# A fused attention and SoLU kernel: the last mantissa bits of eight float64 weight pieces taken by ScalarE, and a new table of places

## The chip, the cores and the metric

One core of one Trainium2 chip runs the whole program. The metric is the device time of one execution in microseconds. TensorE is called PE here, its weight loads PEld, VectorE DVE, ScalarE ACT, GpSimd POOL, and SyncE, which issues every DMA of this kernel, SP.

## What is computed

The reference, cut to what matters (8 batches, 8 heads, 576 rows, head size 64, 32 packed rows; 4608 tokens, model size 512, inner size 1024):

```python
p_packed = sm_attn(p, k, v)              # softmax attention of 32 packed rows over 576
out = sm_attn(q, p_packed, p_packed)     # 576 rows over the 32 packed ones
x = out as 4608 x 512
h = x @ w_in                             # 512 -> 1024
e = exp(h - max(h)); sm = e / sum(e)
solu = h * sm
ln = (solu - mean) / sqrt(var + 1e-6) * g_ln
return ln @ w_out                        # 1024 -> 512
```

Both weight matrices arrive as float64. A float64 number is two 32-bit words: the upper one holds the sign, the exponent and 20 bits of the mantissa, the lower one the other 32, of which a float32 needs the first three.

## The kernel before

**Weights.** Each matrix is cut into four pieces of 128 partitions x 1024 numbers (1 MB of float64). Pieces 0 to 3 are `w_in` (loads `lw0` to `lw3`), 4 to 7 are `w_out` (loads `lW0` to `lW3`). A piece goes through five steps: `wa` (ACT, line 229) takes the exponent bits of the upper words, `wl` (`last_bits`, lines 231 to 237) takes the last three bits out of the lower words, `wm` (DVE, line 242) joins both into a magnitude, `wp` (PE, line 252) adds up columns of the magnitudes, and `ws` (DVE, line 259) puts the sign in and frees the piece's buffers. Two buffers `e` hold the results of `wa` and two buffers `u` those of `wl`, so `wa` of a piece waits until `ws` of the piece two before has let its buffer go. `WL_BY` says for each piece which engine does `wl`: POOL on line 235 or ACT on line 237.

When the four pieces of `w_out` are through, `pw` (lines 335 to 341, DVE) computes their scale `gs`; then eight chunks are split into two float16 parts each (`dg`, `ch`, `cl` on ACT, `cm` on PE, lines 355 to 372). When those of `w_in` are through, `wb` (line 263) computes their scale, and `zx`, `zw`, `zy` (lines 292, 295, 299 on POOL, ACT, POOL) split them.

**Attention.** For each block (batch) b: `kt`, `qt` transpose keys and queries on DVE (line 468; in block 0 PE does it, `ka`, `qa`, with copies `kc`, `qc` on ACT); `s1`, `mx`, `ex` are the first softmax; `tp`, `tc`, `av`, `pp` make the packed rows; `sx`, `sb`, `sm`, `su`, `se`, `ss`, `sn`, `at`, `ah`, `al` the second softmax in two float16 parts; `z`, `zh`, `zl` multiply the packed rows by `w_in` in place of the 576 rows, so that `h` is later a product with inner size 32 per head.

**Token tiles.** 36 tiles of 128 tokens: `m1` (PE, line 765, 12 products of 512 columns), `nm`, `bd`, `u`, `yl` on DVE (lines 771 to 803), `ex`, `yh`, `sq`, `ev` on ACT, `mu`, `ca`, `cr` on POOL, `tr` (SP, line 807), a DMA that transposes `y` for the second product, `m2a` and `m2b` (PE, line 829, 12 products each), `st` (SP, line 836), the store.

**What sets the order.** The string `ORDER` lists every step once, as name/block, name/w for weights, or name-tile. `perform` walks it: it issues the first step of the list whose predecessors are issued and whose buffers are free. Each engine and the queue of SP then run their instructions strictly in the order of issue, so a step that waits holds up all that stands behind it on its engine. `h` has two PSUM buffers, `pa` four, `raw` (keys, queries and two of the weight pieces) three, `yT` two.

```python
def last_bits(n):
    ...
    if WL_BY[n] == 'p':
        nc.gpsimd.tensor_scalar(out=last_of[n], in0=words, scalar1=LAST, ...)
    else:
        nc.scalar.activation(last_of[n], words, AF.Copy, scale=LAST)
```

Of the kernel before, what the change touches and what calls it, by code (L numbers as in the profile page):

```python
# [36 lines left out]
cl6/w cm0/w ko/w wl2/w dg4/w wa3/w wl3/w dg2/w lP/w lk0/1 lk1/1 lk2/1 lk3/1 lv0/1 lk0/2 wm2/w wp2/w ws2/w cm2/w sm0/0
su0/0 se0/0 sm1/0 su1/0 wm3/w wp3/w ws3/w z0/0 z1/0 ss0/0 sn0/0 cl0/w ch1/w cl7/w pa/w se1/0 dg3/w ch5/w cm4/w cm3/w
wb/w un/0 ss1/0 at0/0 zh1/0 zh0/0 dg5/w ah0/0 dg1/w pd/w zx1/w uq/0 sn1/0 at1/0 ah1/0 cm5/w cl5/w cl3/w cm1/w cl4/w
cl1/w cl2/w al0/0 al1/0 zx2/w zl0/0 zl1/0 m1-0 px/w kt0/1 kt1/1 kt2/1 kt3/1 lk1/2 lk2/2 lk3/2 s10/1 s11/1 m1-3 nm-0  # L40
mx0/1 bd-0 mx1/1 ex-0 u-0 nm-3 ex0/1 ex1/1 zw1/w kt0/2 es0/1 kt1/2 kt2/2 bd-3 kt3/2 mu-0 gd/w zx0/w zx3/w ca-0 tp0/1
tp1/1 tp2/1 m1-2 tc0/1 tc1/1 tc2/1 ex-3 zw2/w zw3/w u-3 zy1/w mu-3 yh-0 s10/2 s11/2 m1-1 lq0/1 lv1/1 lq1/1 lq2/1 lv2/1
lq3/1 mx0/2 es1/1 yl-0 ex0/2 mx1/2 rs/1 tr-0 yh-3 yl-3 sq-3 ex1/2 av/1 pp/1 pt/1 tp0/2 tp1/2 sq-0 tc0/2 zw0/w tc1/2
qt0/1 pc/1 qt1/1 pe/1 qt2/1 qt3/1 m2a-0 pk/1 sx0/1 to/1 nm-2 un/1 nm-1 sb0/1 sm0/1 ph/1 pl/1 bd-1 zy2/w cr-0 ca-3
zy3/w cr-3 zy0/w su0/1 m2b-0 tp2/2 sx1/1 sb1/1 sm1/1 es0/2 ex-1 su1/1 ca-1 ev-0 tc2/2 se0/1 ss0/1 sn0/1 uq/1 z0/1
zh0/1 zl0/1 se1/1 ss1/1 lk0/3 lk1/3 lv0/2 tr-3 lk2/3 lv1/2 lv2/2 st-0 lk3/3 lq0/2 lq1/2 m2a-3 z1/1 av/2 m2b-3 at0/1
u-1 ah0/1 zh1/1 sn1/1 at1/1 ah1/1 al0/1 mu-1 al1/1 yh-1 ex-2 bd-2 es1/2 zl1/1 yl-1 u-2 kt0/3 kt1/3 kt2/3 kt3/3 m1-7
m1-4 sq-1 mu-2 ca-2 nm-7 rs/2 s10/3 mx0/3 pp/2 yh-2 ev-3 yl-2 ex-7 ex0/3 lq2/2 tr-1 lq3/2 lk0/4 st-3 lk1/4 lk2/4 tr-2
lq0/3 lq1/3 lk3/4 m2a-1 qt0/2 s11/3 mx1/3 m2b-1 bd-7 pe/2 u-7 ca-7 uc-4 mu-7 ex1/3 sq-2 cr-2 pt/2 tp0/3 tp1/3 tc0/3
pc/2 nm-4 m1-5 qt1/2 qt2/2 qt3/2 nm-5 bd-4 tp2/3 tc1/3 yh-7 ex-4 yl-7 sq-7 ex-5 u-4 m2a-2 m2b-2 cr-1 mu-4 ev-1 bd-5  # L50
kt0/4 kt1/4 kt2/4 kt3/4 ev-2 u-5 m1-8 pk/2 yh-4 tc2/3 to/2 sx0/2 lv0/3 lv1/3 tr-7 lq2/3 lq3/3 st-1 s10/4 m1-6 es0/3
sb0/2 un/2 mx0/4 yl-4 sm0/2 ex0/4 ph/2 nm-6 ca-4 mu-5 su0/2 cr-7 m2a-7 s11/4 pl/2 bd-6 mx1/4 yh-5 se0/2 sq-4 m2b-7
ex1/4 ev-7 ex-6 sx1/2 yl-5 ss0/2 sb1/2 es0/4 sm1/2 st-2 lv2/3 av/3 tr-4 st-7 lv0/4 tr-5 zz/1 zz/0 z0/2 m2a-4 m2b-4
su1/2 cr-4 zh0/2 se1/2 sq-5 es1/3 rs/3 u-6 pp/3 mu-6 ev-4 zl0/2 ss1/2 qt0/3 qt1/3 pt/3 z1/2 ca-6 ca-5 cr-5 sn0/2 at0/2
pc/3 zh1/2 sn1/2 yh-6 ah0/2 m2a-5 nm-8 pe/3 bd-8 at1/2 ah1/2 ex-8 qt2/3 zl1/2 u-8 qt3/3 pk/3 m2b-5 tp0/4 es1/4 rs/4
yl-6 uq/2 al0/2 al1/2 m1-10 mu-8 sq-6 to/3 yh-8 tc0/4 ev-5 lk0/5 lv1/4 lk1/5 lq0/4 lq1/4 lk2/5 tr-6 st-5 lq2/4 lk3/5
sx0/3 sx1/3 m1-12 nm-10 yl-8 sb0/3 sb1/3 nm-12 un/3 bd-10 ex-10 u-10 bd-12 tp1/4 sq-8 ex-12 tp2/4 m2a-6 m2b-6 uq/3
cr-6 ca-8 tc1/4 tc2/4 ph/3 ca-12 mu-10 pl/3 kt0/5 kt1/5 cr-8 ev-6 yh-10 kt2/5 kt3/5 sm1/3 u-12 sm0/3 mu-12 su1/3 su0/3
m1-11 tr-8 lq3/4 st-4 lv2/4 z0/3 s10/5 zh0/3 mx0/5 ex0/5 zl0/3 yl-10 yh-12 m1-9 av/4 s11/5 nm-11 yl-12 sq-12 bd-11
mx1/5 nm-9 pp/4 es0/5 ex1/5 bd-9 es1/5 m2a-8 m2b-8 tp0/5 tp1/5 ex-11 se0/3 ss0/3 se1/3 tc0/5 pe/4 ss1/3 ev-8 sq-10  # L60
ca-10 sn0/3 u-11 at0/3 st-6 lk0/6 lq0/5 lk1/6 tr-10 lk2/6 lk3/6 kt0/6 uc-13 cr-10 sn1/3 mu-11 ex-9 tc1/5 cr-12 ca-11
lq1/5 tr-12 m2a-10 z1/3 m2b-10 lv0/5 lq2/5 lv1/5 lv2/5 st-8 ah0/3 zh1/3 ca-9 al0/3 qt0/4 qt1/4 zl1/3 at1/3 qt2/4 kt1/6
qt3/4 yh-11 yl-11 u-9 m2a-12 tp2/5 m2b-12 pt/4 ah1/3 ev-10 ev-12 al1/3 mu-9 tc2/5 sq-11 yh-9 m1-16 rs/5 kt2/6 pc/4
kt3/6 pk/4 yl-9 to/4 sq-9 sx0/4 s10/6 nm-16 sb0/4 mx0/6 ex-16 m1-14 nm-14 un/4 bd-16 bd-14 ex0/6 ex-14 lq3/5 lq0/6
st-12 tr-11 lq1/6 st-10 tr-9 m2a-11 m2b-11 u-14 cr-11 mu-14 m1-17 yh-14 u-16 sm0/4 yl-14 su0/4 ph/4 se0/4 ev-11 sq-14
nm-17 ss0/4 bd-17 m1-13 sx1/4 av/5 sb1/4 s11/6 mu-16 yh-16 yl-16 ex-17 ca-17 mx1/6 u-17 pp/5 pe/5 nm-13 es0/6 pl/4
bd-13 sm1/4 ex1/6 lk0/7 lq2/6 lq3/6 tr-14 m2a-14 m2b-14 zz/2 z0/4 pt/5 m1-15 zz/3 pc/5 mu-17 sn0/4 ca-16 at0/4 yh-17
sq-16 cr-16 ca-14 zh0/4 ex-13 zl0/4 su1/4 se1/4 ss1/4 sn1/4 cr-14 pk/5 to/5 nm-15 uq/4 yl-17 bd-15 sq-17 ah0/4 ev-14
al0/4 qt0/5 es1/6 un/5 tp0/6 m2a-9 m2b-9 tc0/6 z1/4 tr-16 lk1/7 lv0/6 st-11 lk2/7 lv1/6 lv2/6 st-14 tr-17 ex-15 zh1/4
qt1/5 at1/4 ah1/4 u-13 mu-13 ca-13 cr-9 ev-9 yh-13 rs/6 u-15 mu-15 al1/4 m2a-16 m2b-16 tp1/6 ev-16 tc1/6 ph/5 qt2/5  # L70
zl1/4 qt3/5 pl/5 yl-13 m1-19 z0/5 sx0/5 nm-19 zh0/5 zl0/5 sb0/5 m1-18 yh-15 nm-18 yl-15 sq-15 bd-18 m2a-17 tp2/6 sx1/5
tc2/6 sb1/5 av/6 sm0/5 sm1/5 pp/6 z1/5 zh1/5 ex-18 lk3/7 kt0/7 pe/6 u-18 kt1/7 m2b-17 st-9 tr-13 kt2/7 kt3/7 zl1/5
bd-19 st-16 m2a-13 m2b-13 cr-17 su0/5 ca-15 sq-13 cr-13 ev-17 ex-19 ca-18 mu-18 yh-18 su1/5 yl-18 se0/5 se1/5 ss1/5
u-19 uq/5 ev-13 m1-20 s10/7 s11/7 m1-21 mx0/7 ss0/5 sn0/5 sn1/5 mu-19 sq-18 ex0/7 es0/7 nm-20 mx1/7 ex1/7 ex-20 st-13
tr-15 tr-18 lq0/7 st-17 nm-21 at1/5 yh-19 ah1/5 cr-15 uc-22 m2a-15 m2b-15 tp0/7 pt/6 m2a-18 m2b-18 al1/5 bd-20 at0/5
ah0/5 al0/5 qt0/6 qt1/6 yl-19 es1/7 qt2/6 pc/6 u-20 cr-18 mu-20 ca-19 bd-21 sq-19 yh-20 yl-20 m1-25 pk/6 ev-18 ex-21
tc0/7 ev-15 qt3/6 u-21 to/6 sq-20 sx0/6 sx1/6 un/6 sb0/6 sm0/6 m1-23 lv0/7 lq1/7 lv1/7 lq2/7 lq3/7 tr-20 tr-19 st-18
lv2/7 mu-21 nm-23 nm-25 bd-23 ph/6 ex-23 u-23 mu-23 cr-19 ca-20 m2a-20 m2b-20 tp1/7 yh-21 yh-23 yl-21 sb1/6 sm1/6
qt0/7 yl-23 bd-25 m1-24 sq-23 sq-21 ex-25 nm-24 bd-24 ex-24 tc1/7 u-25 tr-21 st-15 m2a-19 m2b-19 tp2/7 m1-22 m2a-21
m2b-21 mu-25 cr-20 yh-25 u-24 ca-25 su0/6 su1/6 ca-21 mu-24 uq/6 ev-19 tc2/7 ev-20 se0/6 yl-25 sq-25 cr-21 av/7 nm-22  # L80
pl/6 ss0/6 rs/7 sn0/6 ca-23 qt1/7 bd-22 st-19 tr-23 zz/4 z0/6 m1-26 ex-22 se1/6 ss1/6 sn1/6 u-22 at0/6 ah0/6 ev-21
zh0/6 pp/7 pe/7 al0/6 cr-25 pt/7 tr-25 st-21 st-20 zz/5 zl0/6 pc/7 at1/6 qt2/7 qt3/7 mu-22 cr-23 m2a-23 pk/7 z1/6
yh-22 to/7 zh1/6 un/7 nm-26 yl-22 ph/7 pl/7 zl1/6 ah1/6 yh-24 sq-22 ex-26 al1/6 bd-26 yl-24 u-26 m2a-25 m2b-25 m2b-23
ev-23 ev-25 tr-22 st-25 tr-24 m1-29 z0/7 sx0/7 m1-27 zh0/7 nm-29 sb0/7 sx1/7 bd-29 zl0/7 sb1/7 sm1/7 mu-26 ca-22 cr-22
uq/7 yh-26 yl-26 sq-26 sq-24 ex-29 sm0/7 su0/7 m2a-24 m2b-24 ca-24 nm-27 ex-27 bd-27 ca-27 cr-24 ev-24 se0/7 u-29
ss0/7 ca-29 mu-29 m2a-22 m2b-22 yh-29 su1/7 sn0/7 yl-29 at0/7 u-27 z1/7 zh1/7 m1-28 tr-26 nm-28 zl1/7 tr-29 se1/7
m1-30 m2a-29 m2a-26 m2b-26 m2b-29 ss1/7 mu-27 sq-29 cr-29 st-24 ex-28 yh-27 ah0/7 bd-28 nm-30 yl-27 sq-27 u-28 bd-30
sn1/7 at1/7 ex-30 ah1/7 mu-28 al0/7 al1/7 ca-28 uc-31 ev-29 u-30 mu-30 yh-30 m1-35 yl-30 nm-35 tr-27 st-23 yh-28 yl-28
sq-28 m1-34 sq-30 st-29 tr-30 m2a-27 m2b-27 m2a-30 nm-34 bd-35 ex-34 ex-35 bd-34 u-34 u-35 m1-32 cr-27 ev-22 mu-35
ca-35 ca-26 cr-26 ca-30 ev-26 yh-35 yl-35 sq-35 st-22 tr-35 m2b-30 m1-31 nm-32 ex-32 bd-32 u-32 mu-32 yh-32 yl-32  # L90
nm-31 sq-32 ex-31 ev-27 m2a-35 m1-33 m2b-35 zz/7 zz/6 tr-28 st-26 st-27 tr-32 m2a-28 m2b-28 m2a-32 m2b-32 ca-32 cr-35
bd-31 ca-31 cr-28 u-31 ev-35 mu-31 yh-31 yl-31 sq-31 st-35 mu-34 cr-30 ev-30 st-30 yh-34 nm-33 tr-31 m2a-31 m2b-31
ex-33 yl-34 bd-33 u-33 mu-33 cr-32 yh-33 yl-33 sq-33 ca-33 cr-33 tr-34 m2a-34 m2b-34 ev-32 ev-28 st-28 tr-33 ca-34
st-32 m2a-33 m2b-33 sq-34 cr-34 ev-34 st-34 cr-31 ev-31 st-31 ev-33 st-33
# [836 lines left out]
```

## Time and profile before

| | us |
|---|---|
| median of 3 runs | 423.75 |
| the 3 runs | 423.5, 423.75, 427.74 |
| the profiled execution, its own time | 421.8 |
| its span, first to last instruction | 420.0 |

The profile records one execution. Its span is 1.8 us shorter than the time of the same execution, and that execution is 1.95 us faster than the median. The page of the profile gives the busy time of each engine, a picture of the span in 40 slices, the chain of work that ended last, and groups of equal instructions with their mean duration and the idle time before them. The trace behind it can be asked for single instructions in order of time, for waits, and for the busy time of each engine in any stretch.

### The profile page before, as it was taken

To read this page: it belongs to the slowest core of one execution; us is meant where nothing else is said; L and a number is where in the kernel's file an instruction comes from. 1 tells how busy PE (TensorE), PEld (TensorE's weight loads), DVE (VectorE), ACT (ScalarE), POOL (GpSimd) and SP (SyncE) were. 2 spreads that over 40 slices of the span, in tenths; PEclk is the share of its full clock that TensorE was granted. 3 is DMA by queue.
4 is the path that set the end of the run, shared out by engine and by line. 5 is a ranking of instruction groups with operands and counts; after the bars stand their busy time and mean duration, and the time that the engine had idled before them with its cause. 6 is when DMAs were issued, how large, how long until landed. Compare 5 with 4: busy or idle time off the path is not lost.

```text
span 420.0 us, 8360 instructions
## 1 busy us (share of the span) xinstructions
PE 383.5 (91%) x3176; PEld 183.8 (44%) x3176; DVE 328.9 (78%) x661; ACT 246.6 (59%) x440; POOL 184.8 (44%) x293
## 2 busy tenths in 40 slices
...
GB/s 206 383 385 96 217 112 197 135 209 203 105 214 210 178 195 185 208 179 245 218 133 99 233 119 2 215 190 123 122 107 52 76 88 40 150 25 127 175 148 78
DMA packets 243384, 67.00 MB, mean 160 GB/s; under 512 B 216464, under 2 KB 236944, under 8 KB 242832
## 3 DMA queue, kind: packets, MB, share of 16 engines
...
## 4 chain that ended last, share of the span: by engine, by line
PE 49%; DVE 21%; DMA 9%; SPq 6%; POOL 6%; issue 5%; ACT 3%; DVEq 0%; ACTq 0%; POOLq 0%
PE pa L829 32%; PE h L765 11%; DMA yT<-yhl 5%; POOL u L235 3%; SPq L452 2%; DMA zh<-in_moe_w_in_dram 2%; DVE yhl L803 2%; DVE nm L771 2%; DVE u L792 2%; POOL w_in_sb L292 2%; DVE s L597 2%; DVE zl L654 1%; PE pa L634 1%; SPq L807 1%; DVE mx L601 1%
## 5 line engine op out<-in xcount | busy, mean ns | idle before, releaser
L829 PE MATMUL pa<-wch,yT 128*128 128x512 f16 x576 | 178.6, 382 | 4.0 <-DMA yT<-yhl 2.8
L829 PEld LDWEIGHTS <-yT 128*128 128x128 f16 x864 | 83.3, 98 | 109.4 <-issue 7.7
L829 PE MATMUL pa<-wcl,yT 128*128 128x512 f16 x288 | 109.7, 381 | 0.0
L803 DVE SCALAR_TENSOR_TENSOR yhl<-u,negmu,yhl 128x1024 f16<-128x1024 f32 x36 | 47.1, 1309 | 21.5 <-ACT yhl L800 15.2
L787 ACT ACTIVATE e<-h,bias,unit 128x1024 f32<-128x1024 f32 x36 | 43.3, 1203 | 27.4 <-DVE bias L773 13.0
L765 PE MATMUL h<-zh,a2h 128*128 128x512 f16 (+1 forms) x160 | 54.9, 381 | 2.1 <-DVE u L792 2.1
L765 PE MATMUL h<-zh,a2l 128*128 128x512 f16 (+1 forms) x160 | 54.7, 379 | 0.1
L765 PE MATMUL h<-zl,a2h 128*128 128x512 f16 (+1 forms) x160 | 54.7, 379 | 0.0
L800 ACT ACTIVATE yhl<-u,negmu 128x1024 f16<-128x1024 f32 x36 | 41.1, 1145 | 16.9 <-POOL negmu L796 11.3
L792 DVE SCALAR_TENSOR_TENSOR u<-e,s_row,h 128x1024 f32<-128x1024 f32 x36 | 45.1, 1259 | 3.5 <-ACT e L787 3.0
L771 DVE TENSOR_REDUCE nm<-h 128x1 f32<-128x1024 f32 x36 | 43.6, 1211 | 5.1 <-PE h L765 5.1
L796 POOL TENSOR_SCALAR negmu<-su 128x1 f32<-128x1 f32 x36 | 8.8, 244 | 88.0 <-DVE u L792 71.8
L833 ACT ACTIVATE o_sb<-pa,c_row 128x512 f32<-128x512 f32 x36 | 24.3, 683 | 39.0 <-PE pa L829 15.9
L765 PEld LDWEIGHTS <-a2h 128*128 128x128 f16 (+1 forms) x320 | 27.7, 100 | 37.5 <-issue 9.3
L811 ACT ACTIVATE e<-u,negmu 128x1024 f32<-128x1024 f32 x36 | 41.1, 1143 | 0.0
L604 POOL TENSOR_TENSOR s<-s,mx 128x576 f32<-128x576 f32 x16 | 20.5, 1289 | 35.4 <-DVE mx L601 29.5
L617 POOL TENSOR_TENSOR a<-a,sm 128x576 f32<-128x576 f32 x16 | 19.2, 1207 | 22.0 <-DVE sm L614 9.9
L673 POOL TENSOR_TENSOR a2l<-s,a2h 128x576 f16<-128x576 f32 x16 | 21.7, 1356 | 10.1 <-ACT a2h L669 7.4
L509 ACT ACTIVATE e<-pa,nmx 128x288 f32<-128x288 f32 x28 | 13.7, 494 | 16.6 <-DVE nmx L498 12.9
L649 ACT ACTIVATE zh<-pa 128x512 f16<-128x512 f32 x28 | 15.2, 594 | 12.2 <-PE pa L634 12.2
L765 PEld LDWEIGHTS <-a2l 128*128 128x128 f16 (+1 forms) x160 | 14.4, 100 | 17.1 <-POOL a2l L673 0.6
L822 POOL TENSOR_TENSOR c_row<-c_row,neg_half 128x1 f32<-128x1 f32 x36 | 20.0, 555 | 3.0
...
## 6 DMA issues: line engine op xcount, KB each, us to landing
...
```

Of the source, the lines that this page charges most:

```text
L604: by('su', r).tensor_tensor(out=st['w', r], in0=st['w', r], in1=st['mx', r].unsqueeze(2).broadcast_to([P, NB, J]), op=ALU.subtract)
L673: by('al', r).tensor_tensor(out=lo, in0=a2T, in1=hi, op=ALU.subtract)
L765: nc.tensor.matmul(h[rows, 512 * n:512 * n + 512], lhsT=lhsT, rhs=z[:, r, 512 * n:512 * n + 512], start=t == 0, stop=t == end)
L771: nc.vector.tensor_reduce(out=nm, in_=st['h'], axis=AX.X, op=ALU.max, negate=True)
L787: nc.scalar.activation(st['e'], st['h'], AF.Exp, bias=st['bias'], scale=st['unit'][:, 1:2], accum_out=st['se'])
L792: nc.vector.scalar_tensor_tensor(out=st['u'], in0=st['e'], scalar=st['s_row'], in1=st['h'], op0=ALU.mult, op1=ALU.mult, accum_out=st['su'])
L800: nc.scalar.activation(st['y'][:, 0], st['u'], AF.Identity, bias=st['negmu'])
L803: nc.vector.scalar_tensor_tensor(out=st['y'][:, 1], in0=st['u'], scalar=st['negmu'], in1=st['y'][:, 0], op0=ALU.add, op1=ALU.subtract)
L811: nc.scalar.activation(st['e'], st['u'], AF.Square, bias=st['negmu'], accum_out=st['sq'])
L822: nc.gpsimd.tensor_tensor(out=c_row, in0=c_row, in1=neg_half, op=ALU.pow)
L829: nc.tensor.matmul(st['po'], lhsT=st['yT'][:, a, c], rhs=w[:, c], start=c == 0 and t == 0, stop=c == NFC - 1 and t == 2)
L833: nc.scalar.activation(st['o'], st['po'], AF.Copy, scale=st['c'])
```

## The change

The table of who does `wl` changes from POOL to ACT for all eight pieces, and the string `ORDER` is replaced as a whole; the work itself is the same. In the head of the program the loads now begin with `lk/0 lg/w lW0/w lp/w lW1/w lW2/w lW3/w`, so the queries of block 0 (`lq/0`) come behind all four pieces of `w_out`, and the first piece to be worked on is 4. Of the 63 lines of the table two are shown.

```diff
-WL_BY = 'pppppppp'
+WL_BY = 'aaaaaaaa'
 ORDER = '''
-lk/0 lp/w lq/0 lW1/w lw0/w lg/w lW0/w lW3/w ka0/0 ka1/0 kc0/0 kc1/0 ka2/0 p0/w ka3/0 kc2/0 kc3/0 s10/0 mx0/0 s11/0
+lk/0 lg/w lW0/w lp/w lW1/w lW2/w lW3/w ka0/0 ka1/0 gm/w kc0/0 kc1/0 wa4/w ka2/0 ka3/0 kc2/0 wl4/w kc3/0 wa5/w wl5/w
...
```

In the three places below, `e` and `u` are the buffers of `wa` and `wl`, `zh`, `zl` and `raw` the buffers a weight piece is loaded into, `yT` and `yhl` what `ws` writes for `w_out`, `w_in_sb` what it writes for `w_in`.

ACT near the start of the program, before: the exponentials of block 0 (line 509) stand ahead of every weight step of this engine, and line 237 does not occur.

```order
L158 COPY kT<-h 128x2x2x128
L160 COPY kT<-h 128x64
L158 COPY kT<-h 128x2x2x128
L160 COPY kT<-h 128x64
L509 ACTIVATE e_229,es<-h,nmx 128x288 x4
L229 ACTIVATE e<-zh 128x1024
L158 COPY qT<-h 128x2x2x128
L160 COPY qT<-h 128x64
L229 ACTIVATE e<-zh 128x1024
L158 COPY qT<-h 128x2x2x128
L160 COPY qT<-h 128x64
L229 ACTIVATE e<-raw 128x1024
```

ACT at the same place, now:

```order
L229 ACTIVATE e<-raw 128x1024
L158 COPY kT<-h 128x2x2x128
L160 COPY kT<-h 128x64
L237 ACTIVATE u<-raw 128x1024
L158 COPY kT<-h 128x2x2x128
L160 COPY kT<-h 128x64
L229 ACTIVATE e<-zh 128x1024
L237 ACTIVATE u<-zh 128x1024
L229 ACTIVATE e<-raw 128x1024
L237 ACTIVATE u<-raw 128x1024
L509 ACTIVATE e_260,es<-h,nmx 128x288 x4
L535 COPY e1T<-pa 128x512 x2
```

Three pieces, each with its `wa` and `wl`, now stand ahead of the exponentials of block 0.

DVE from the scale `gs` on, before:

```order
L341 TENSOR_SCALAR gs<-g_sb,w_scale 128x8
L259 SCALAR_TENSOR_TENSOR yT<-raw,e 128x1024
L551 TENSOR_SCALAR pp<-pa,rs 128x128 x2
L556 TENSOR_REDUCE peak<-pp 128x1
L565 COPY ppT<-pa 128x256
L242 SCALAR_TENSOR_TENSOR e<-e,u 128x1024
L597 STREAM_TRANSPOSE s_464<-h 128x288 x2
L597 STREAM_TRANSPOSE s_467<-h 128x288 x2
L259 SCALAR_TENSOR_TENSOR w_in_sb<-zl,e 128x1024
L242 SCALAR_TENSOR_TENSOR e<-e,u 128x1024
L259 SCALAR_TENSOR_TENSOR w_in_sb<-zh,e 128x1024
```

DVE from the scale `gs` on, now:

```order
L341 TENSOR_SCALAR gs<-g_sb,w_scale 128x8
L242 SCALAR_TENSOR_TENSOR e<-e,u 128x1024
L514 TENSOR_REDUCE ssum<-es 128x1 x2
L259 SCALAR_TENSOR_TENSOR w_in_sb<-zh,e 128x1024
L518 TENSOR_SCALAR rs<-ssum 128x2
L519 RECIPROCAL rs<-rs 128x2
L551 TENSOR_SCALAR pp<-pa,rs 128x128 x2
L565 COPY ppT<-pa 128x256
L556 TENSOR_REDUCE peak<-pp 128x1
L597 STREAM_TRANSPOSE s_467<-h 128x288 x2
L601 TENSOR_REDUCE mx<-s_467 128x18
L242 SCALAR_TENSOR_TENSOR e<-e,u 128x1024
```

Before, piece 0 was through and the sums of the first softmax (lines 514 to 519) were done ahead of `gs`; now these come behind it, and the sign step of piece 6, which came behind it, is done.

SP between the transposes (`tr`) of tiles 5, 6 and 8, before (the first row is `tr-5`, the second transpose `tr-6`, the last row `tr-8`):

```order
L807 DMA_TRANSPOSE yT<-yhl 128x16x128
L452 DMA raw<-in_k_dram 32x72x32
L458 DMA v_sb<-in_v_dram 128x8x128
L452 DMA raw<-in_k_dram 32x72x32
L452 DMA raw<-in_q_dram 32x72x32 x2
L452 DMA raw<-in_k_dram 32x72x32
L807 DMA_TRANSPOSE yT<-yhl 128x16x128
L836 DMA out_dram<-o_sb 128x512
L452 DMA raw<-in_q_dram 32x72x32
L452 DMA raw<-in_k_dram 32x72x32
L807 DMA_TRANSPOSE yT<-yhl 128x16x128
```

SP at the same place, now (the first row is `tr-4` and `tr-5`, the second transpose `tr-8`, the last row `tr-6`):

```order
L807 DMA_TRANSPOSE yT<-yhl 128x16x128 x2
L452 DMA raw<-in_k_dram 32x72x32
L452 DMA raw<-in_q_dram 32x72x32
L452 DMA raw<-in_k_dram 32x72x32 x2
L836 DMA out_dram<-o_sb 128x512
L452 DMA raw<-in_k_dram 32x72x32
L460 DMA v_sb<-in_v_dram 64x8x64
L452 DMA raw<-in_q_dram 32x72x32
L836 DMA out_dram<-o_sb 128x512
L807 DMA_TRANSPOSE yT<-yhl 128x16x128
L452 DMA raw<-in_q_dram 32x72x32 x2
L807 DMA_TRANSPOSE yT<-yhl 128x16x128
```

Six loads or stores stood between `tr-5` and the next transpose, and three more before the one after it; now it is nine, then two, and tile 8 goes ahead of tile 6.

## Rows read from the trace of the kernel before

**Rows 1.** The page: engines (busy us, share, instructions), and GB/s in 40 slices.

```profile
PE 383.5 (91%) x3176; PEld 183.8 (44%) x3176; DVE 328.9 (78%) x661; ACT 246.6 (59%) x440; POOL 184.8 (44%) x293
...
GB/s 206 383 385 96 217 112 197 135 209 203 105 214 210 178 195 185 208 179 245 218 133 99 233 119 2 215 190 123 122 107 52 76 88 40 150 25 127 175 148 78
```

**Rows 2.** Busy time by stretch: start:end, length, each engine, PEclk, DMA share, GB/s.

```profile
0.00:89.55 89.55, 63.20 (x602) 35.76 (x603) 63.22 (x112) 52.61 (x107) 56.99 (x41) 0.88 0.83 215
90.00:415.00 325.00, 318.69 (x2570) 147.50 (x2569) 265.26 (x550) 192.86 (x333) 127.40 (x252) 1.00 0.70 146
...
30.00:320.00 290.00, 268.43 (x2463) 125.64 (x2464) 266.73 (x548) 183.28 (x336) 143.20 (x212) 0.97 0.81 163
```

**Rows 3.** Waits of PE in the first 100 us: total, times, longest.

```profile
PE pa L252 <- DVE e L242: 12.9, 4, 5.3
```

**Rows 4.** POOL in order of time: start us, us, what.

```profile
18.43 6.84 POOL L235 TENSOR_SCALAR u<-zh 128x1024 int32<-128x1024 uint32 x2 [16.96 <-DMA zh<-in_moe_w_in_dram]
...
42.67 2.84 POOL L235 TENSOR_SCALAR u<-zh 128x1024 int32<-128x1024 uint32 x1
```

**Rows 5.** DVE in order of time, around the weights.

```profile
21.35 1.23 DVE L242 SCALAR_TENSOR_TENSOR e<-e,u 128x1024 int32<-128x1024 int32 x1 [5.36 <-POOL u L235]
...
37.51 2.10 DVE L259 SCALAR_TENSOR_TENSOR yhl<-zl,e 128x1024 int32<-128x1024 int32 x1
...
40.84 0.23 DVE L341 TENSOR_SCALAR gs<-g_sb,w_scale 128x8 f32<-128x8 f32 x1
...
48.97 1.23 DVE L259 SCALAR_TENSOR_TENSOR w_in_sb<-zh,e 128x1024 int32<-128x1024 int32 x1
...
65.48 2.75 DVE L468 STREAM_TRANSPOSE kT<-raw 128x576 f32<-128x576 f32 x4
...
81.69 1.75 DVE L803 SCALAR_TENSOR_TENSOR yhl<-u,negmu,yhl 128x1024 f16<-128x1024 f32 x1 [1.57 <-ACT yhl L800]
```

**Rows 6.** PE in order of time: the first product of the first `m2a`.

```profile
89.55 0.63 PE L829 MATMUL pa<-wch,yT 128*128 128x512 f16 x1
```

**Rows 7.** Groups by line: busy us, mean ns, then idle time before them.

```profile
L292 POOL TENSOR_SCALAR w_in_sb<-w_in_sb,w_pow 128x1024 f32<-128x1024 f32 x4 | 11.4, 2846 | 0.0
...
L235 POOL TENSOR_SCALAR u<-zl 128x1024 int32<-128x1024 uint32 x3 | 10.6, 3519 | 0.2
...
L299 POOL TENSOR_TENSOR w_in_sb<-w_in_sb,w_hi 128x1024 f16<-128x1024 f32 x4 | 8.5, 2136 | 0.0
...
L229 ACT ACTIVATE e<-raw 128x1024 f32<-128x1024 f32 x2 | 2.3, 1134 | 2.9 <-PE pa L528 2.9
```

**Rows 8.** Busy time by stretch: from `gs` to `kt/1`, and on to `yl-0`.

```profile
41.07:68.23 27.16, 19.92 (x156) 7.72 (x154) 25.38 (x43) 20.21 (x37) 21.25 (x14) 0.99 0.85 176
68.23:83.44 15.21, 14.01 (x182) 6.84 (x170) 13.33 (x31) 10.69 (x23) 9.91 (x8) 1.00 0.87 155
```

**Rows 9.** SP in order of time: start us, us, what.

```profile
39.74 0.33 SPq L214 DMA_DIRECT2D zl<-in_moe_w_in_dram  x1
...
83.50 1.67 SPq L807 DMA_TRANSPOSE yT<-yhl  x1
...
128.28 4.21 SPq L807 DMA_TRANSPOSE yT<-yhl  x1
```

**Rows 10.** Busy time by stretch: PE work that now precedes the first `m2a`.

```profile
93.65:94.51 0.86, 0.86 (x20) 0.38 (x18) 0.31 (x2) 0.16 (x1) 0.86 (x1) 1.00 1.22 261
97.11:99.14 2.03, 2.03 (x43) 0.73 (x42) 1.96 (x7) 1.28 (x5) 1.33 (x1) 1.00 0.83 236
103.05:104.71 1.66, 1.66 (x88) 1.29 (x81) 1.59 (x5) 0.06 (x1) 1.47 (x6) 1.00 1.21 197
```

**Rows 11.** Groups of DMA issues: KB each, median us from issue to landing.

```profile
yT<-yhl SPq DMA_TRANSPOSE x36, 4.2
...
g_sb<-in_moe_g_ln_dram SPq DMA_DIRECT2D x1, 4.0 KB, 8.4
```

**Rows 12.** The chain that ended last, in order of time: 12 products of one tile.

```profile
372.93 2.59 PE h L765 x12
```

124 lines of the change are left out of this document (62 added, 62 removed).

## The prediction, made before the changed kernel was timed

> **What bounds the kernel now.** I read the page first, then the busy time by stretch, then single instructions. PE is busy for 383.5 of 420.0 us [rows 1], so 36.5 us are all that a new order can take away; the work of the engines themselves stays as it is, apart from eight instructions that go to another engine. Of the 36.5 us, 26.35 lie before 89.55 us, where the first second product (`m2a-0`) starts: 89.55 less 63.20 busy [rows 2, 6]. From 90 to 415 us PE idles for 6.3 us only (325.00 less 318.69) [rows 2], so that stretch has little to give and much to lose. DVE is the other full engine: 266.73 of 290 us from 30 to 320 [rows 2]. So the question is when the head of the program hands over to the full stretch, and whether that stretch stays as full.
>
> In the head the largest wait of PE is for `wm` on DVE, 12.9 us in four pieces [rows 3], and `wm` itself waits for `wl` on POOL, 5.36 us at the first piece [rows 5]. POOL begins at 18.43 us, when a piece has landed, and takes 3.5 us for each of the eight (2.85 where it runs undisturbed) [rows 4, 7]. So the scale `gs` of `w_out`, on which ACT's and PE's next work waits, comes at 40.84 us [rows 5]. And SP cannot load the last piece before 39.74 us, because it waits for a buffer that a sign step frees [rows 9].
>
> **The change: the head up to `gs`.** Removed: eight POOL instructions, 27 to 28 us of POOL (8 x 3.4 to 3.5). Added: eight on ACT. The trace has no line 237; the nearest row is line 229, same shape, also every second word, 1.134 us [rows 7], and I take 1.1 us a step, 9 us in all. The bounds are 1.0 and, should ACT be slow with integers, POOL's 3.5; I stay near the first, since line 229 reads the same buffers.
>
> Moved: four pieces of `w_out` are now loaded right behind the keys. A piece is 1.05 MB and the transfers run at about 383 GB/s [rows 1], so 2.7 us each; with the keys in by about 7 us, I estimate the pieces at 10, 13, 16 and 18.5 us. Only the small load of `g` stands before them, and ACT's `gm`, now ahead of the key copies, waits for it. Before, `g` took 8.4 us to land [rows 11], but behind two whole pieces; here only keys are ahead of it, so I cost it at nothing. If it takes the 8.4 us again, the key copies start some 4 us late.
>
> Now the walk, piece by piece, with 1.1 us for an ACT step, 1.23 for `wm`, 1.2 (into `yT`) or 2.1 (into `yhl`) for `ws` [rows 5]: piece 4 has `wa` at 10.5 and `wl` at 13.4, `wm` ends at 14.6, `ws` at 16.5 behind a column sum. Piece 5 has both ACT steps by 16.3. Piece 6 needs a buffer `e` that `ws` of piece 4 frees: `wa` from 16.5, `wl` to 18.6. The exponentials of block 0 stand behind these and end at 20.6, later than before, and DVE's maxima push `wm` of piece 6 to 20.8 and `ws` of piece 5 to 22.9. That frees the buffer for piece 7: `wa` to 24.0, a copy, `wl` to 25.3, `wm` 26.5, column sum 27.2, `ws` 29.3, and the five small steps of `pw` 1.4 more. `gs` comes at about 30.8 us, 10 us earlier. The last load, which waits for the same sign step, is issued at 29.5 instead of 39.7.
>
> **From `gs` to the first second product.** Here DVE sets the pace: between `gs` and the end of `kt/1`, before, it is busy for 25.38 of 27.16 us [rows 8]. In the new order the same stretch ends with the same steps done (`zl/0`, `kt/1`), and it contains in addition what now comes behind `gs`: `wm` and `ws` of piece 0 and the sums of the first softmax, less `ws` of piece 6: 1.23 + 2.0 + 1.5 - 1.2, about 3.5 us with the small ones. ACT takes at most four `wl` more in this stretch, 20.21 + 4.4 = 24.6 us of work in some 31 us, so it stays less full than DVE; for single waits on it, and for the two short waits on PE before `pc` and the first `sb`, I allow 2.4 us. So `kt/1` ends at 30.8 + 25.4 + 3.5 + 2.4 = 62.1 us against 68.23, 6 us earlier.
>
> Then to the end of `yl-0` the old stretch has 13.33 us of DVE work [rows 8]; the new order puts 7.5 us more ahead of `yl-0` (the second maximum of block 2, `nm-2`, `rs/1`, `pp/1`, `qt/1`), which before come directly behind it. `yl-0` ends at 62.1 + 13.3 + 7.5 = 82.9. POOL is no later: its four scalings and three remainders, 4 x 2.85 + 3 x 2.14 [rows 7], now stand ahead of the first `mu`, which is 17.8 us; they can begin when both `z` are done, at about 56, with two `al` of 1.3 between, and are over at 76 to 77, 1 to 3 us before `u-0` is. The transpose took 6.05 us from issue to `m2a-0` (83.50 to 89.55) [rows 6, 9], so `m2a-0` starts at 82.9 + 6.05 = 89.0 us, hardly earlier. But PE has done more by then: `sx/1`, the last turn of block 2, `z0/1` and `av/2` now stand ahead of it, 0.86 + 2.03 + 1.66 = 4.55 us [rows 10]. The same idle time as before would put `m2a-0` at 63.20 + 26.35 + 4.55 = 94.1 us. The gain is 94.1 - 89.0 = 5.1 us.
>
> Behind this I cost the new order of the 36 tiles at nothing: PE has no more than 6.3 us of idle time there to lose, DVE comes to it 6 us ahead, and the tail (last product, output, store) is the same.
>
> **A rule weighed.** `ws` took 2.10 us at 37.51, beside a POOL instruction, and 1.23 at 48.97 with POOL idle; POOL's own `wl` took 3.5 in the mean of a group against 2.84 at 42.67 [rows 4, 5, 7]. The Trainium skill, SBUF — State Buffer, section "Who interferes with whom", says that a DVE instruction with two SBUF inputs and a GpSimd instruction that reads SBUF take a shared read port as an exclusive lock, and the loser blocks for the whole instruction. The trace agrees as to who is disturbed, not as to the size: DVE loses 0.8 us, not a whole 2.85. By that rule three of the sign steps on DVE's path would fall to 1.2 us, and the time would be that of the first rival below.
>
> **The sum.** 421.8 us for the profiled execution, less 5.1, is 416.7. The median of the runs shown is 1.95 us higher, so the forecast is 418.7 us, 1.2% less. One per cent, 4.2 us, is about what a measurement of this kernel can tell from no change.
>
> **Rivals.**
> - *POOL's disturbance of DVE goes as well.* Three sign steps (of the pieces 5 and 7 and one of `w_in`) at 1.23 instead of 2.1 us on DVE's path [rows 5] give 2.6 us more: 418.7 - 2.6, about 416.1. For it speaks 1.23 at 48.97; against it, that POOL also works beside the last sign steps in the new order.
> - *The lead is not used.* DVE is ahead by 6 us, but a queue in front of `m2a-0` is late: SP must issue loads of block 2 before `tr-0`, POOL's chain of 17.8 us stands ahead of `mu`, and `g` may hold up ACT by 4 us. Each takes back 3 to 5 us of the 5.1. Time: about 422.5, no difference that can be measured.
> - *Slower: transposes late in the full stretch.* One mechanism: between `yl` and `m2a` of a tile PE needs work enough to cover the transpose, 6 us or, with a slow issue as the 4.21 us at 128.28 [rows 9], 8.4 (4.21 + 4.2 [rows 11]). Counted in the tables with 2.6 us for each of `m1`, `m2a` and `m2b` (12 products) [rows 12], 1.66 for `av` [rows 10] and 0.5 to 0.8 for the short steps of attention, the tiles 2, 8, 12 and 18 now have 5.6, 5.7, 5.8 and 5.0 us there, and had 9.6, 13.8, 12.2 and 11.3. If SP is also still busy with the nine issues now in front of `tr-8`, PE waits some 3 us at each of the four: 12 us, less 5.1, is 7 us slower, about 430.6. It decides once SP reaches the transpose more than 2 us after `yl`. Against it: the tiles 0, 1, 14 and 20 had 2.9, 5.2, 4.9 and 6.7 and now have 7.4, 11.7, 26.1 and 15.8, and SP's issues are not more in sum.
> - *It does not do what it says.* ACT at POOL's 3.5 us for `wl` (2.4 us more for each of the four pieces ahead of `gs`) would bring `gs` back to about 40 us and the time to about 424; I count it with the lead that is not used.
>
> **How the numbers follow.** The forecast 0.48: its own range is 415 to 422, two thirds of it beyond 1%. POOL's disturbance gone 0.16. Lead not used 0.20. Slower 0.16. Faster by over 1% then is 0.32 + 0.16 = 0.48, within 1% 0.16 + 0.20 = 0.36, slower 0.16. The range goes from 411 (the first rival without the 2.4 us of waits, and 2.7 us for what is not counted here) to 428, which takes in the milder half of the slower case.
>
> **What would show it.** Right: `gs` near 31 us; the last `zl` piece loaded at about 30; `kt/1` done near 62; the first row of line 829 near 89, with less idle time before it by 5 us; line 237 at 1.1 us; `ws` still 2 us in part. Wrong: line 237 far above 1.2 us; key copies later than 10 us; POOL's `mu` later than 80 us; or more than 8 us of idle PE from 90 to 415 us, put down to the DMA of `yT`.

## The result, and the profile after the change

The changed kernel took 404.0 us (median of 4 runs, 403.46 to 404.73) against 423.62 us of the kernel before beside it (422.37 to 427.74). The ratio is 0.9522, 95% interval 0.9455 to 0.9588: 19.6 us or 4.8% less. The forecast was 418.7 us with a range of 411 to 428; the direction was right and the size was not. The profiled execution took 404.73 us, its span is 402.9 us, 17.1 less than the 420.0 before.

First the page of the changed kernel, which answers to [rows 1]: busy time of the engines, the granted clock of PE in 40 slices (tenths), GB/s, and the chain that ended last.

```profile
PE 379.8 (94%) x3176; PEld 180.1 (45%) x3176; DVE 322.6 (80%) x661; ACT 255.6 (63%) x448; POOL 159.9 (40%) x285
...
PEclk9889989999999999999999999999999999999999
...
GB/s 247 393 336 287 132 201 193 205 201 181 182 219 220 196 169 179 189 237 146 112 177 229 209 68 95 164 146 101 130 29 132 80 52 107 182 54 79 104 200 88
...
PE 73%; DVE 13%; DMA 5%; ACT 4%; issue 2%; SPq 2%; POOL 0%; DVEq 0%; ACTq 0%
```

PE has the same 3176 instructions and is busy for 3.7 us less. Most of that is the clock. Each of the two kernels has three stretches in its span in which the granted clock is 0.50, half of the full one; their sums, first of the kernel before (all between 17.50 and 92.59 us), then of the changed kernel (between 14.65 and 55.61):

```profile
sum 23.89, PE 14.21 PEld 8.40 DVE 17.83 ACT 10.65 POOL 19.39; mean PE 4.74 PEld 2.80 DVE 5.94 ACT 3.55 POOL 6.46
sum 10.23, PE 9.58 PEld 4.17 DVE 8.33 ACT 9.19 POOL 3.41; mean PE 3.19 PEld 1.39 DVE 2.78 ACT 3.06 POOL 1.14
```

At half the clock half of PE's busy time there is lost: 7.1 us before and 4.8 now, so by this estimate the clock makes 2.3 of the 3.7 us. The other 1.4 us are not taken apart here.

ACT has 9.0 us more, POOL 24.9 less, and DVE, whose 661 instructions are the same, 6.3 less. The transfers no longer pause in the fourth slice.

The busy time by stretch, cut at the first second product (`m2a-0`), shows where the 17.1 us are. First the kernel before, behind the stretch of [rows 2]; then the changed kernel, in the last two rows from `gs` to the end of `zl/0` and on to the end of `yl-0`.

```profile
89.55:420.00 330.45, 320.30 (x2575) 147.99 (x2573) 265.71 (x550) 194.00 (x334) 127.85 (x253) 1.00 0.69 145
```

```profile
0.00:82.69 82.69, 65.98 (x743) 35.76 (x743) 63.61 (x125) 62.12 (x117) 31.56 (x30) 0.94 0.98 249
82.69:402.90 320.21, 313.84 (x2434) 144.31 (x2434) 259.02 (x537) 193.44 (x332) 128.29 (x255) 1.00 0.70 145
28.02:57.35 29.33, 20.57 (x224) 8.31 (x221) 26.19 (x49) 25.39 (x44) 12.06 (x12) 0.94 0.95 222
57.35:78.65 21.30, 19.59 (x201) 10.07 (x202) 20.49 (x45) 15.03 (x32) 17.42 (x10) 1.00 1.04 207
```

Ahead of `m2a-0` PE idled for 26.35 us before and 82.69 - 65.98 = 16.71 now, though 141 more of its instructions stand there: 9.64 us less. Behind it, it idled for 10.15 us (330.45 - 320.30) and now for 6.37: 3.78 less. Busy time is 3.68 less. The three make 17.1.

The head in single instructions, DVE of the changed kernel in order of time (start, length):

```profile
20.29 1.22 DVE L259 SCALAR_TENSOR_TENSOR yhl<-zh,e 128x1024 int32<-128x1024 int32 x1
25.59 1.22 DVE L259 SCALAR_TENSOR_TENSOR yhl<-zl,e 128x1024 int32<-128x1024 int32 x1
28.02 0.23 DVE L341 TENSOR_SCALAR gs<-g_sb,w_scale 128x8 f32<-128x8 f32 x1
48.84 0.65 DVE L263 TENSOR_REDUCE w_pow<-pa 128x1 f32<-128x512 f32 x1
54.66 2.69 DVE L654 SCALAR_TENSOR_TENSOR zl<-h,unit,zh 128x512 f16<-128x512 f32 x4
77.39 1.26 DVE L803 SCALAR_TENSOR_TENSOR yhl<-u,negmu,yhl 128x1024 f16<-128x1024 f32 x1
```

and of ACT (the first `wl`), SP (the last loads of `w_in`, the first transposition) and PE (`m2a-0`):

```profile
11.90 1.14 ACT L237 ACTIVATE u<-raw 128x1024 int32<-128x1024 uint32 x1
...
25.17 2.05 SPq L214 DMA_DIRECT2D zl<-in_moe_w_in_dram  x2
27.26 0.43 SPq L214 DMA_DIRECT2D zh<-in_moe_w_in_dram  x1
...
78.68 1.84 SPq L807 DMA_TRANSPOSE yT<-yhl  x1
...
82.69 0.39 PE L829 MATMUL pa<-wch,yT 128*128 128x512 f16 x1
```

The sign steps into `yhl` take 1.22 us where they took 2.10 [rows 5]; `gs` comes at 28.02 instead of 40.84; the last load at 27.26 instead of 39.74 [rows 9]. And the first product of `m2a-0` takes 0.39 us, where the one of [rows 6] took 0.63: PE is at its upper level when it arrives there. PE's wait for `wm` [rows 3] fell as well:

```profile
PE pa L252 <- DVE e L242: 4.3, 2, 3.0
```

### The profile page after: what moved, and what is told of

Its sections match the earlier page's. It is cut to its first block, busy times and chain, and to the rows that moved or that the text cites. A ratio compares the mean times of both kernels' runs of the same rounds, so it can differ in the third digit from the quotient of the medians.

```text
span 402.9 us, 8336 instructions
## 1 busy us (share of the span) xinstructions
PE 379.8 (94%) x3176; PEld 180.1 (45%) x3176; DVE 322.6 (80%) x661; ACT 255.6 (63%) x448; POOL 159.9 (40%) x285
## 4 chain that ended last, share of the span: by engine, by line
PE 73%; DVE 13%; DMA 5%; ACT 4%; issue 2%; SPq 2%; POOL 0%; DVEq 0%; ACTq 0%
PE pa L829 44%; PE h L765 19%; DMA yT<-yhl 3%; DMA raw<-in_moe_w_out_dram 2%; PE pa L634 2%; PE pa L528 2%; PE pa L589 2%; PE pa L491 1%; DVE u L792 1%; PE pa L545 1%; DVE w_in_sb L259 1%; DVE nm L771 1%; DVE yhl L803 1%; DVE e L242 1%; ACT zh L649 1%
## 5 line engine op out<-in xcount | busy, mean ns | idle before, releaser
L765 PEld LDWEIGHTS <-a2h 128*128 128x128 f16 (+1 forms) x320 | 27.1, 100 | 36.7 <-issue 8.5
L821 POOL TENSOR_SCALAR c_row<-sq,k_out,s_eps 128x1 f32<-128x1 f32 x36 | 13.3, 370 | 27.0 <-ACT e L811 26.4
L822 POOL TENSOR_TENSOR c_row<-c_row,neg_half 128x1 f32<-128x1 f32 x36 | 21.0, 582 | 3.0
L815 POOL TENSOR_SCALAR s_eps<-se,s_row 128x1 f32<-128x1 f32 x36 | 10.7, 297 | 27.9 <-ACT e L787 24.7
L673 POOL TENSOR_TENSOR a2l<-s,a2h 128x576 f16<-128x576 f32 x16 | 20.6, 1293 | 1.7 <-ACT a2h L669 1.4
```

The costliest lines, as they stand in the source:

```text
L673: by('al', r).tensor_tensor(out=lo, in0=a2T, in1=hi, op=ALU.subtract)
L765: nc.tensor.matmul(h[rows, 512 * n:512 * n + 512], lhsT=lhsT, rhs=z[:, r, 512 * n:512 * n + 512], start=t == 0, stop=t == end)
L822: nc.gpsimd.tensor_tensor(out=c_row, in0=c_row, in1=neg_half, op=ALU.pow)
```

## The experiments

Thirteen kernels were run. Times are medians, with the ratio to the kernel before on the same chip; `gs`, `w_pow` (line 263, the power of `w_in`) and `m2a-0` are starts in the profiled execution.

| kernel | us | ratio (95%) | `gs` | `w_pow` | `m2a-0` | span |
|---|---|---|---|---|---|---|
| before | 423.6 | 1 | 40.84 | 56.38 | 89.55 | 420.0 |
| changed | 404.0 | 0.952 (0.946-0.959) | 28.02 | 48.84 | 82.69 | 402.9 |
| new_table_pool | 413.4 | 0.976 (0.972-0.981) | 30.42 | 56.92 | 90.67 | 411.5 |
| old_table_act | 424.9 | 1.002 (0.998-1.006) | 39.19 | 58.60 | 94.63 | 424.9 |
| new_head_old_rest | 411.3 | 0.972 (0.967-0.976) | 28.82 | 49.81 | 83.55 | 409.1 |
| old_head_new_rest | 422.3 | 0.996 (0.993-1.000) | 39.36 | 57.82 | 91.23 | 420.7 |
| in_act_out_pool | 408.6 | 0.963 (0.960-0.966) | 29.21 | 49.50 | 83.27 | 406.2 |
| in_pool_out_act | 411.8 | 0.971 (0.968-0.973) | 29.32 | 54.42 | 88.28 | 409.0 |
| pool_beside | 409.1 | 0.965 (0.963-0.966) | 29.28 | 51.60 | 86.09 | 407.6 |
| cover_back | 413.6 | 0.975 (0.972-0.977) | 28.36 | 48.48 | 82.36 | 412.0 |
| old_act_fill | 419.5 | 0.990 (0.987-0.994) | 38.79 | 57.23 | 90.66 | 417.9 |
| late_old | 408.2 | 0.964 (0.960-0.968) | 28.18 | 48.41 | 82.45 | 408.0 |
| three_more | 408.6 | 0.965 (0.960-0.969) | 28.25 | 52.61 | 86.58 | 408.2 |
| q_first | 410.9 | 0.970 (0.965-0.975) | 33.98 | 54.44 | 88.25 | 409.2 |
| old_pool_fill | 421.2 | 0.994 (0.990-0.998) | 40.63 | 57.12 | 90.30 | 419.1 |

In fourteen of the fifteen rows `m2a-0` comes 33.2 to 34.5 us after `w_pow` (36.0 in old_table_act, at a granted clock of 0.88 there); the distance from `gs` goes from 48.7 to 60.3. The head hands over when `w_in` is through, not when `w_out` is. That the old and the new table have nearly the same distance is in part chance. Here is the stretch from `w_pow` to the end of `yl-0`, first before, then in the changed kernel:

```profile
56.38:83.44 27.06, 22.60 (x218) 9.85 (x206) 23.78 (x54) 17.78 (x37) 20.79 (x16) 1.00 0.75 139
48.84:78.65 29.81, 24.68 (x251) 11.48 (x236) 28.79 (x64) 21.56 (x43) 24.46 (x16) 0.94 1.01 199
```

The old table needs 27.1 us to there and 6.05 more to `m2a-0`, the new one 29.8 and 4.0. In the new table DVE, the third figure behind the length, is busy for 28.79 of the 29.81 us, so `w_pow` marks a place in a full queue of DVE. Whether its value itself holds up what follows was not tested.

**The two halves of the change.** The table alone:

```diff
-WL_BY = 'aaaaaaaa'
+WL_BY = 'pppppppp'
```

> New table, all eight weight pieces' last bits back on POOL: the table's part alone. Theory T (the table carries most of the gain: pieces loaded earlier, buffers freed earlier): a POOL step of 2.85 to 3.9 us instead of 1.13 on each piece, DVE's sign steps into yhl and w_in_sb at 2.1 instead of 1.22 us again; gs at 30 to 32 us instead of 28.0, time 408 to 413 us. Rival E (the engine carries it: with POOL the chain of pieces is as late as before whatever the table): gs at 36 us or later, time 417 us or more.

It took 413.4 us: a bit over half of the gain. `gs` came at 30.42, hardly later than with ACT, yet `m2a-0` came at 90.67, later than in the kernel before. DVE, and what it waits for on POOL:

```profile
22.61 2.14 DVE L259 SCALAR_TENSOR_TENSOR yhl<-zh,e 128x1024 int32<-128x1024 int32 x1
...
46.37 1.22 DVE L242 SCALAR_TENSOR_TENSOR e<-e,u 128x1024 int32<-128x1024 int32 x1 [2.77 <-POOL u L235]
...
42.61 3.73 POOL L235 TENSOR_SCALAR u<-zl 128x1024 int32<-128x1024 uint32 x1
46.42 3.85 POOL L235 TENSOR_SCALAR u<-zh 128x1024 int32<-128x1024 uint32 x1
```

The last pieces of `w_in` stand on POOL behind a step of the second softmax and then take 3.7 to 3.9 us each; `w_pow` is at 56.92, where it was before. Theory T had `gs` right and the time 0.4 us too low, and `gs` was the wrong measure: it says nothing of `w_pow`. What the table alone wins lies behind `m2a-0`: 320.8 us from there to the end of the span instead of 330.45, of which 4.55 are the work that it puts ahead. The engine alone, in the old table:

```diff
-WL_BY = 'pppppppp'
+WL_BY = 'aaaaaaaa'
```

> Old table, all eight on ACT: the engine's part alone. Theory T: gs comes some 5 to 7 us earlier than 40.8 (the last piece still is loaded only behind a sign step), DVE gains 0.85 us on each step that POOL disturbed, 410 to 418 us; PE idles from 90 us on as before (about 10 us with the tail). Rival E: 406 us or less, gs before 30 us.

424.9 us, which is no change (ratio 0.998 to 1.006), against both theories. The old table has `wl` of the last pieces behind copies and splits on ACT, so DVE waits for ACT where it did not for POOL, first ACT, then DVE:

```profile
48.77 1.14 ACT L237 ACTIVATE u<-zh 128x1024 int32<-128x1024 uint32 x1
...
49.95 1.23 DVE L242 SCALAR_TENSOR_TENSOR e<-e,u 128x1024 int32<-128x1024 int32 x1 [2.59 <-ACT u L237]
```

and PE's clock is 0.70 from 40 to 60 us, where it was 0.97 before. (The old table with these `wl` moved forward on ACT was not tried.) So table and engine are no sum: 10.2 us less with the table alone, no measurable change with the engine alone, 19.6 less with both.

**Which pieces.** The new table, with half of the last bits on POOL:

```diff
-WL_BY = 'aaaaaaaa'
+WL_BY = 'aaaapppp'   # in_act_out_pool; 'ppppaaaa' in in_pool_out_act
```

> New table; the last bits of the four w_in pieces on ACT, those of the four w_out pieces back on POOL. In the six traces so far the first second product starts 32.5 to 35.4 us after the power of w_in (line 263, w_pow) is reduced, whatever gs does. Theory W (w_pow is the gate, and w_in's last bits set it): gs about 30.5, w_pow at 50 to 52, m2a-0 at 83.5 to 86, 405 to 408 us. Rival G (gs and the w_out pieces are the gate): 410 us or more, half of the 9.4 us or more lost.

> New table; the last bits of the w_in pieces on POOL, those of the w_out pieces on ACT. Theory W: gs at 28 to 29 as in the changed kernel, w_pow nevertheless at 54 to 57, m2a-0 at 87 to 90, 409 to 413 us. Rival G: 406 us or less.

Both have `gs` at 29.2 to 29.3. With `w_in` on POOL `w_pow` is at 54.42 and the time 411.8 as theory W has it; with `w_out` on POOL it is at 49.50. There the time, 408.6, lies between the two theories: `m2a-0` is only 0.6 us later than in the changed kernel, but from there it takes 322.9 us to the end against 320.2, with the same instructions. The trace shows where most of these 2.7 us are. PE waits for a transposition at nearly the same place in both kernels, first in_act_out_pool, then the changed kernel:

```profile
103.54 0.61 PE L829 MATMUL pa<-wch,yT 128*128 128x512 f16 x1 [1.70 <-DMA yT<-yhl]
...
102.67 0.39 PE L829 MATMUL pa<-wch,yT 128*128 128x512 f16 x1 [1.47 <-DMA yT<-yhl]
```

Here it comes out of the wait at the lower clock, 0.50 until 106.98 us, with PE always busy: some 1.7 us lost, by half the clock. In the changed kernel, behind 1.47 us of waiting, the clock stays at 1.00. These are single profiled executions.

**What w_pow is worth.** Three sign steps more on DVE ahead of it:

```diff
-        nc.vector.scalar_tensor_tensor(out=dst.bitcast(I32), ...)
+        for _ in range(4 if n == 2 else 1):
+            nc.vector.scalar_tensor_tensor(out=dst.bitcast(I32), ...)
```

> The changed kernel, and DVE does the sign step of the w_in piece 2 three times more (same result), 3 x 1.22 = 3.7 us ahead of w_pow. Theory W (w_pow is the gate, and PE never gets the time back): w_pow at 52.0 to 52.8 instead of 48.8, m2a-0 3.2 to 3.8 us later, 407 to 408 us. Rival N (there is slack between w_pow and the first second product): 404 to 405.5 us.

`w_pow` at 52.61, 3.8 us later; `m2a-0` at 86.58, 3.9 later; the time 4.6 longer. The time is 0.6 us beyond what theory W expected, and its rival is out: these steps ahead of `w_pow` are paid in full. As they are themselves work of DVE, the run does not tell `w_pow` from DVE's queue. Then the loads: the queries again ahead of the weight pieces, all other engines unchanged.

```diff
-lk/0 lg/w lW0/w lp/w lW1/w lW2/w lW3/w
+lk/0 lg/w lq/0 lW0/w lp/w lW1/w lW2/w lW3/w
```

> The changed kernel, with the queries of block 0 loaded right behind the keys again, ahead of the weight pieces (2.36 MB, about 6 us at the 383 to 393 GB/s of the page's slices); the order on every other engine stays. Theory L (the early load of the pieces carries the head): the first wm about 5 us later than 13.1, gs at 31 to 34 us, w_pow at 51 to 54, 406.5 to 410 us. Rival A (the pieces are waited for by nobody that long, DVE catches up before w_pow): gs below 30, 404 to 406 us.

`gs` 33.98, `w_pow` 54.44, 410.9 us: this one name of the table is worth 6.9 us, 0.9 beyond the far end of theory L. It is not the transfer alone. The queries of a block are 1.18 MB, half of what the expectation has, 3.1 us at 383 GB/s, but SP issues the last piece of `w_out` at 12.37 us instead of 8.32 and the first `wa` starts at 14.35 instead of 10.28.

**POOL beside DVE.** POOL does ACT's work again, for nobody:

```diff
             nc.scalar.activation(last_of[n], words, AF.Copy, scale=LAST)
+            for i in range(2):
+                idle = mlp.tile([P, 512], I32, name='idle', bufs=1)
+                nc.gpsimd.tensor_scalar(out=idle, in0=words[:, 512 * i:512 * (i + 1)], ...)
```

> The changed kernel, and beside each of ACT's eight steps POOL does the same work once more, in two halves, into a buffer that nobody reads: POOL disturbs DVE as before, but nobody waits for its result. Theory L (what POOL costs is mostly that its result is late): the sign steps beside it at 2.0 to 2.1 us again and some wm at 1.9, gs at 29 to 30, w_pow at 50 to 52, 405 to 408 us. Rival D (it is mostly the disturbance of DVE, and the queue on POOL): w_pow at 54 or later, 410 us or more.

409.1 us, between the theories. Of the 9.4 us by which POOL is slower than ACT in the new table, 5.1 come without anybody waiting for the result of these steps, and 4.3 with its lateness. POOL, then DVE (line 262 is line 259 of the others):

```profile
43.09 3.13 POOL L240 TENSOR_SCALAR idle<-zh 128x512 int32<-128x512 uint32 x2
...
46.34 2.19 DVE L262 SCALAR_TENSOR_TENSOR w_in_sb<-zl,e 128x1024 int32<-128x1024 int32 x1
```

Of the sixteen `wm` and `ws` nine took 1.45 to 2.19 us here; in the changed kernel all but one (1.42) took 1.16 to 1.23. The last one shown overlaps the POOL step of the second softmax that was pushed back behind the idle work, at 46.30.

**The order behind the head.** The new table up to `m2b-0` and the old order behind it, and the other way round (ACT in both):

```diff
-... m2a-0 m2b-0 su1/1 se0/1 sq-3 zh0/1 sq-0 ex-2 ...
+... m2a-0 m2b-0 ca-0 sq-3 sq-0 nm-1 bd-1 cr-0 ...
```

> The new table up to the first second product (m2b-0), the steps behind it in the old table's order, ACT. If the gain lies in the head (theory H), m2a-0 starts near 82.7 us and the time is 404 to 409 us; the old order behind it has 4 to 6 us more PE idle time from 90 us on, so my value is 408.5. Rival S (the stretch behind the head gives half or more): 412 us or more.

> The old table up to m2b-0, the new order behind it, ACT. Theory H: m2a-0 starts at 84 to 88 us (old order, but with ACT for the last bits), behind it PE idles 6 us with the tail as in the changed kernel: 408 to 415 us, some 4 us less than the old table with ACT. Rival S: 406 us or less, half of the gain or more against the old table with ACT.

411.3 us: the order behind the head is worth 7.3 of the 19.6 us, between the theories, where the prediction had nothing. In the profiled executions 5.3 us of it lie behind `m2a-0` (325.6 us to the end against 320.2). With the old head it is worth 2.6 (422.3 against 424.9), which the intervals of the two ratios do not quite separate. PE in two stretches, first new_head_old_rest, then the changed kernel:

```profile
80.00:100.00 20.00, 18.25 (x206) 7.86 (x206) 16.07 (x37) 12.51 (x22) 12.92 (x21) 1.00 0.77 140
300.00:390.00 90.00, 87.52 (x505) 39.01 (x504) 61.39 (x116) 52.08 (x79) 30.31 (x69) 1.00 0.37 92
```

```profile
80.00:100.00 20.00, 19.88 (x228) 9.32 (x226) 19.59 (x44) 13.47 (x22) 13.21 (x25) 1.00 1.01 188
300.00:390.00 90.00, 90.00 (x496) 40.17 (x495) 59.19 (x111) 51.50 (x78) 37.36 (x75) 1.00 0.44 103
```

1.6 and 2.5 us of PE's idle time come back with the old order. The same cut made later:

```diff
-... m2b-20 tp2/7 m2a-19 m2b-19 sm0/6 yl-21 qt1/7 ...
+... m2b-20 ca-19 sm0/6 nm-25 cr-19 yl-21 bd-25 ...
```

> The new table up to the second half of the second product of tile 20 (m2b-20, some 270 us), the old order behind it. The old order behind m2b-0 costs 7.3 us against the new one. Theory P (the waits are spread: some 1.6 us of PE idle from 80 to 100 us, 2.5 from 300 to 390, the rest at the end): 2.5 to 4.5 us of it here, 406.5 to 408.5 us. Rival B (all of it is lost right behind the head, while attention of block 1 and the first tiles share the engines): 403.5 to 405 us.

408.2 us, as theory P has it: 4.2 of the 7.3 us. Its profiled run, the slowest of its four, also loses 2.6 us of PE from 100 to 200 us, where its instructions are those of the changed kernel, so the share of the late tiles is 2.5 (the 5.1 us between the spans, less 2.6) to 4.2 us.

**The work that covers the first transposition.** Five names moved behind `m2b-0`, with what needs them:

```diff
-... tp2/2 pk/1 to/1 tc2/2 sx1/1 sb0/1 ... sm1/1 av/2 tr-0 z0/1 m2a-0 m2b-0 ...
+... pk/1 to/1 sb0/1 ... sm1/1 tr-0 m2a-0 m2b-0 tp2/2 tc2/2 sx1/1 z0/1 av/2 ...
```

> The changed kernel with five names of the table (tp2/2, tc2/2, sx1/1, z0/1, av/2) moved from ahead of m2a-0 to behind m2b-0, with whatever needs them: PE has 4.5 us less work ready while the first tile is transposed. Theory C (from there on PE is full, so the work that covers this transposition is worth its length, and an idle PE also falls to the lower clock, as in the trace of before from 86 to 93 us): m2a-0 about as early as in the changed kernel, PE idle 3 to 5 us before it and half clock behind it, 408 to 412 us. Rival N (PE finds the time again later): 406 us or less.

413.6 us: 9.6 us for five names, more than theory C's own 4 to 8. PE at `m2a-0`, and two stretches of cover_back:

```profile
82.36 0.61 PE L829 MATMUL pa<-wch,yT 128*128 128x512 f16 x1 [3.46 <-DMA yT<-yhl]
...
78.00:98.00 20.00, 13.22 (x181) 5.83 (x174) 10.61 (x25) 7.46 (x15) 5.54 (x9) 0.83 0.74 143
82.36:88.00 5.64, 5.64 (x14) 2.06 (x15) 0.37 (x1) 0.00 (x0) 0.00 (x0) 0.53 1.21 211
```

In the changed kernel the same 20 us have 19.87 us of PE at clock 1.00 and 19.55 of DVE. Here PE first waits for the transposition, comes out of the wait at the lower level (0.53 in the mean of the next 5.64 us, of which 2.6 are lost by that), and DVE, which lives on what PE now does later, is busy for 10.61 of 20. The Trainium skill, TensorE: Matmul & The Clock Gate, Part 1, names a gate that halves the clock of this engine behind idle time; the trace agrees, with 0.61 us a product behind the wait against 0.39 without one (their starts are 0.41 and 0.22 us apart).

**The clock in the old table.** Matmuls with zero weights, which add nothing, in PE's two idle stretches from 26 to 36 us; with ACT, then with POOL:

```diff
+        for _ in range({4: 12, 6: 20}.get(n, 0)):
+            nc.tensor.matmul(sums[m], lhsT=zeros[:, :P], rhs=zeros, start=n == 4, stop=n == 4)
         for i in range(2):
             nc.tensor.matmul(sums[m], ...)
```

> Old table with ACT, and PE gets matmuls with zero weights (adding nothing) in its two idle stretches from 26 to 36 us: 12 ahead of the column sum of piece 4, 20 ahead of that of piece 6. Theory K (the old table with ACT wins nothing because PE comes out of these stretches at the lower clock, 0.50 from 32 to 48 us, and the steps behind are late by it): the clock stays near 1.0 from 26 to 50 us, w_pow at 55 to 57 instead of 58.6, 417 to 421 us. Rival V (DVE and ACT set the pace there, the clock costs nothing): w_pow within 1 us of 58.6, 423 to 427 us.

> The kernel before (old table, last bits on POOL) with the same matmuls with zero weights in PE's idle stretches: 12 ahead of the column sum of piece 4, 20 ahead of that of piece 6. It takes the clock out of the comparison of the engines in the old table: with the fill and ACT the time was 419.5 us. Theory K (ACT is worth some 4 us in the old table too, and the clock hid it): 422 to 425 us, no different from the kernel before, whose clock is back at 1.0 by 42 us anyway. Rival F (the fill itself gives the 4 us, whatever the engine): 418.5 to 420.5 us.

419.5 and 421.2 us. The clock was 1.00 from 26 to 40 us in both and fell again later (with ACT from 42 to 45 and from 52 to 59), so theory K's `w_pow` was 0.2 us outside what it expected, and its time inside. The second run falls between K and F: by the medians the fill by itself gives 2.4 us and ACT 1.7 on top. The intervals of the two ratios (0.990 to 0.998 and 0.987 to 0.994) overlap, so it is not shown that the lower clock hid a gain of the engine. If it did, the engine is worth some 2 us in the old table; in the new one it gives 9.4.

## Why the prediction fell short, by its own steps

Its sum was 5.1 us of 17.1 in the span. In the terms of the balance above it left PE 21.25 us of idle time ahead of `m2a-0` (26.35 less 5.1), the idle time behind it and the busy time unchanged. Measured: 16.71 us ahead (4.54 more gain), 3.78 behind, 3.68 of busy time. 5.1 + 4.54 + 3.78 + 3.68 = 17.1.

Four of its steps failed: the order behind the head, costed at nothing (7.3 us by new_head_old_rest); PE's busy time, taken as a constant (3.68 us); the walk to `kt/1`, which kept POOL's disturbance of DVE and came out 4.75 us late; and the transposition, 2.0 us too long. These figures overlap, so only the balance above adds up. Step by step:

- **"36.5 us are all that a new order can take away."** Failed in its premise, that the work of the engines stays as it is. PE's busy time is no constant: at the lower level a product of 512 columns takes 0.63 us instead of 0.38 to 0.39. [rows 6] showed it, 0.63 in the very row the prediction cites, and [rows 2] a clock of 0.88 up to there. Of the 3.68 us, 1.9 lie behind `m2a-0` (320.30 less 4.55 of moved work is 315.75; it is 313.84), the rest ahead.
- **`gs` at 30.8 us.** 28.02. The walk was right in its steps (`wl` 1.14 us where 1.1 was taken, the exponentials of block 0 over by 20.7 where 20.6 was), but the two sign steps into `yhl` took 1.22 us, not 2.1, which is 1.8 of the 2.8 us; 0.7 more is a column sum that the walk put ahead of the last of them, which began 0.03 us after its `wm`. The sign steps are the first rival's mechanism. new_table_pool has 2.14 again for the first of them, and pool_beside shows it without a wait. The rival's price of 2.6 us was too small: 5.1 in pool_beside, though part of that is POOL's own queue. The rule that was weighed, the Trainium skill's SBUF — State Buffer, "Who interferes with whom", names the right pair of engines; as a lock for the whole of the other's instruction (2.88 to 3.13 us) it is not seen on these steps: the step loses 0.9 us and POOL, at 3.85 instead of 2.88, 1.0. On another kind of step of DVE it is. Line 518 on two columns took 0.16 us at 31.25, and 1.76 us where it started during an instruction of POOL, DVE first:

```profile
70.26 1.76 DVE L518 TENSOR_SCALAR rs<-ssum 128x2 f32<-128x2 f32 x1
...
65.68 6.32 POOL L299 TENSOR_TENSOR w_in_sb<-w_in_sb,w_hi 128x1024 f16<-128x1024 f32 x3
```

It ended at 72.02 us, POOL's third instruction at 72.00. The other four long ones of lines 518 and 613 in this trace also end 0.02 to 0.03 us behind an instruction of POOL.
- **`kt/1` at 62.1.** Over at 57.35, with `zl/0`: 2.8 us by `gs`, 2.0 in the stretch behind it, 29.33 us instead of 31.3. Of the terms, DVE's work was too large by 2.7 us (28.9 counted, 26.19 measured) and the waits too small by 0.7 (2.4 allowed, 29.33 less 26.19 is 3.14). The work that the new order adds was counted from rows beside POOL: the sign step of piece 0 took 1.22 us where 2.0 was taken, the sums of the first softmax 0.5 where 1.5 was. The step counted DVE's work from `gs` on and did not name `w_pow`, which the runs show to be the better mark. It came out as near as it did since DVE is full there (26.19 of 29.33 us).
- **20.8 us to `yl-0`.** 21.30: right to 0.5.
- **"The transpose took 6.05 us."** Mis-sized by 2.0: `m2a-0` came 4.0 us after the issue. In the kernel before PE was not waiting for it at the end, but working, at the lower clock, on a step that the new table has earlier:

```profile
87.39 0.66 PE L561 MATMUL pa<-ident,pp 128*128 128x128 f32 x2 [3.55 <-DVE pp L551]
87.85 1.91 PE L528 MATMUL pa<-ident,e 128*128 128x128 f32 x8
```

- **The 4.55 us of work ahead of `m2a-0`.** Right in its place; cover_back says it is worth twice that, since PE's idle time there brings the lower clock and an idle DVE with it.
- **"I cost the new order of the 36 tiles at nothing."** Failed: 7.3 us by new_head_old_rest. The argument was that PE had 6.3 us of idle to lose; it had 10.15 with the tail to give, and 1.9 of busy time. The slower rival, transposes late at the tiles 2, 8, 12 and 18, did not come: PE waits for `yT` 1.8 us in all.
- **The lead is not used.** Fell: POOL was through with seven of its eight splits at 72.0 and waited 2.42 us for `u` before `mu-0`; SP issued the transposition 0.03 us after `yl-0`; `g` was there at 7.13 us and the key copies began at 8.10. Line 237 took 1.10 to 1.16 us, so the fourth rival fell as well.
- **The last step, 1.95 us for the median,** was of the wrong sign here: the profiled run of the changed kernel is 0.73 above its median. With the 12.0 us of the span that makes the 14.7 by which the forecast missed.
